# q for two groups at a time, w1 in one block of columns, outputs picked by one masked product and one sum, four unit products fewer

## The chip, the cores and the metric

The kernel runs on one core of one Trainium2 chip. A core has a matrix engine (PE; its weight loads are shown as PEld), a vector engine (DVE), an engine for activation functions (ACT), GpSimd (POOL) and an engine that here only issues transfers (SP). They work side by side and wait for each other through semaphores. 16 DMA engines bring data from HBM into the on-chip memory (SBUF, 128 partitions); PE writes its results into eight banks of PSUM. The metric is the device time of one execution in microseconds, lower is better; the time before is a median of three runs.

## The reference

Two layers, each an attention step of a decoder with cached keys and values and a gated feed-forward, on 4 sequences with one token each:

```python
B, D, Hq, Hkv, Sk, Dh, F = 4, 512, 32, 8, 4096, 128, 1792
def A(x, k_cache, v_cache, wq, wo):
    q = (x @ wq).reshape(B, 1, Hq, Dh).transpose(0, 2, 1, 3)
    k, v = repeat(k_cache, 4, axis=1), repeat(v_cache, 4, axis=1)
    p = softmax(einsum("bhqd,bhkd->bhqk", q, k) * Dh ** -0.5)
    return einsum("bhqk,bhkd->bhqd", p, v).transpose(0, 2, 1, 3).reshape(B, 1, Hq * Dh) @ wo
def F_(x, w1, w3, w2):
    return (silu(x @ w1) * (x @ w3)) @ w2
for layer in range(2):
    x = x + A(layernorm(x), k_cache, v_cache, wq, wo)
    x = x + F_(layernorm(x), w1, w3, w2)
```

Both layers use the same weights and the same caches, all in float32. Keys and values are 4 x 8 x 4096 x 128 numbers each, 134 MB together; a layer needs them once.

## The kernel before

**Loads.** The host lays keys, values and all weights side by side into one array `rows` of 128 partitions. The table `LOADS` lists 87 transfers from it into one large SBUF tile, `space`, as (first unit, count, place), a unit being 256 columns of float32. `pump` (L125) issues them in that order, on SP, each as soon as its places are free; `done` (L158) frees places after the last instruction that reads them, and calls `pump`. SP runs in order: a transfer whose place is not free holds back all behind it. Some data of layer 0 stays in `space` for layer 1 (w1, half of the last group's keys and values, part of wq, wo and w2), and layer 1 goes through the groups in reverse.

**Attention.** A group is one of the 8 key heads with its 4 query heads. Per group (loop at L587) `score` multiplies the keys of 2048 positions with q (16 tiles of 512 columns for 4 sequences, four row blocks of 32 side by side on PE), `maximum` and `exponent` take the softmax of it without its division, `turn` transposes p into pT, all this twice; then `weigh` multiplies the values (twice 16 matmuls into the two banks `o_ps[0]` and `o_ps[1]`). `join_maxima` and `join_sums` make the factors that put the partial softmaxes together, and `finish` (L424) picks the four blocks that belong together out of each bank, one factor and one DVE instruction per block: four of bank 0 stand beside the second `weigh`, four of bank 1 behind it. `turn_o` and `gather_o` stand inside the next group's scores, after 8 and after 12 of its 16 matmuls.

**q.** While a group runs, q of the next one is made: `share_q` (four matmuls of the four 128-row pieces of x, into the four row blocks of the bank `wide`), `take_q` (one DVE pass that scales them), `turn_q` (four matmuls that add the pieces and transpose, within the second scores), `copy_q` (into `qT`).

**Feed-forward** (L480). w1 and w3 stand in two blocks of columns, "a" (256) and "b" (192); 4 x 4 matmuls each fill one block of the banks `gate` and `up`. `swish` is a sigmoid on ACT and a product on DVE, `times_up` another product, `turn_h` transposes h, `down` multiplies w2, 14 chunks of 16 small matmuls. `hum` multiplies a unit matrix into a bank that nothing reads; `busy` does the same at the end of an attention. `factor` makes the reciprocal deviation of the layer norm: matmuls that sum squares (`mean`, L233), one DVE instruction (L256), one on POOL (L257).

The order on each engine is the order of the code. A tile is the unit of the waits that are put in: an instruction that writes a tile waits for readers of other parts of it, where the engine has not waited for a later one yet.

Of the kernel before, what the change touches and what calls it, by code (L numbers as in the profile page):

```python
# [15 lines left out]
REP = HQ // HKV  # L16
# [54 lines left out]
SCRATCH = 64  # L71

# [5 lines left out]
def tile_decode_layers(ctx: ExitStack, tc: tile.TileContext, rows, out):  # L78
# [29 lines left out]
    for kind, n in (("w1a", KC), ("w1b", KC), ("w3a", KC), ("w3b", KC), ("w2", 14)):  # L108
        stream += [(kind, k) for k in range(n)]
    size = {"wq": HOME, "wo": HOME, "kv": U // KB, "w2": D // KB}  # L110
    for kind in ("w1", "w3"):
        size[kind + "a"], size[kind + "b"] = 4 * HALF // KB, 4 * (FJ - HALF) // KB
# [45 lines left out]
    def done(layer, *key):  # L158
        if layer == 0 and (key[0][:2] == "w1" or key[0] in ("wq", "wo") and key[1] >= HELD or key[:2] == ("kv", TURN) and key[2] in KEPT or key[0] == "w2" and key[1] >= LASTS):
            return  # L160
# [18 lines left out]
    rowsum, ssq, ve, rstd = columns[:, 4:5], columns[:, 5:6], columns[:, 6:8], columns[:, 8:10]  # L179
    alike, other = columns[:, 12:12 + REP], columns[:, 12 + REP:12 + 2 * REP]  # L180
# [13 lines left out]
    qT = const.tile([P, B, 32 + LEAD], F32, name="qT")  # L194
    nc.vector.memset(qT, 0.0)
    sums_ps = psum.tile([P, KC, P], F32, name="sums_ps")
# [40 lines left out]

    def deviation():
# [7 lines left out]
    def lay_down(xin):  # L246
        xT = work.tile([P, P], F32, name="xT", bufs=1)
        nc.vector.transpose(xT, xin)
        return xT
# [9 lines left out]
    def layernorm():  # L259
        xc, sq = deviation()  # L260
        xT = lay_down(xc)
# [7 lines left out]
        return xT, factor  # L269
# [9 lines left out]
    def turn_over(g):  # L279
        xT = lay_down(x_ps)  # L280
# [3 lines left out]
        for k in range(KC):  # L284
            for i in range(KC):
                nc.tensor.matmul(q_ps[32 * i:32 * i + 32, :].rearrange("p (h c) -> p h c", h=REP),
                                 xT[:, 32 * k:32 * k + 32], w[:, k, i], start=(k == 0), stop=(k == KC - 1))
# [4 lines left out]
        nc.vector.tensor_scalar(qT[:, :, LEAD:].rearrange("p b (t r) -> p b t r", t=2)[:, :, :, 0:REP],  # L292
                                q.unsqueeze(2).to_broadcast([P, B, 2, REP]), SCALE, None, op0=ALU.mult)
        xc, sq = deviation()
        xT = lay_down(xc)
        squares(xc, sq)

        def factor():
# [4 lines left out]
            inverse(rstd, o_ps[1][:, 1:3])  # L303

        return xT, factor


    def copy_q(q=None):
        q = misc[:, 0:B * REP].rearrange("p (h b) -> p b h", h=REP) if q is None else q
        nc.vector.tensor_copy(qT[:, :, LEAD:].rearrange("p b (t r) -> p b t r", t=2)[:, :, :, 0:REP],  # L310
                              q.unsqueeze(2).to_broadcast([P, B, 2, REP]))
# [11 lines left out]
    def take_q(rstd):  # L323
        shares = work.tile([P, REP * DH], F32, name="shares", tag="p", bufs=1)
        nc.vector.tensor_scalar(shares, wide, rstd, -D * SCALE, op0=ALU.mult, op1=ALU.mult)  # L325
# [9 lines left out]
    def score(layer, g, c, between={}):  # L335
        ps = scores()
        order = (2, 3, 4, 5, 6, 7, 0, 1) if layer and (g, c) == (TURN, STORED) else range(TILES)
        for m, r in enumerate(order):
            key = "kv", g, TILES * c + r
            t = loaded(*key)  # L340
            at = LEAD - REP * (r // 2)
# [338 lines left out]
```

## Time and profile before

| | |
|---|---|
| median of 3 runs | 702.99 us (702.89 to 703.22) |
| the profiled execution | 703.43 us |
| its span, first to last instruction | 701.6 us |
| mean granted clock of PE | 0.827 |
| read from HBM | 296.81 MB, 423 GB/s over the span |
| busiest line of PE | L349, scores: 164.8 us in 1024 records |
| second | L413, values: 151.0 us in 1024 records |

The page gives busy time per engine, the transfers per queue, the chain of work that ended last, and groups of equal instructions as: line, engine, operation, output <- inputs, shape, count | busy us, mean ns of one | idle time of the engine before them, and what ended it. A matmul of float32 stands as two records with a weight load each. Granted clock is the share of full speed at which PE ran. In a timeline row the first two numbers are start and duration in us, and the bracket is the idle time before it and what ended that.

### The profile page before, as it was taken

To read this page: it belongs to the slowest core of one execution; us is meant where nothing else is said; L and a number is where in the kernel's file an instruction comes from. 1 tells how busy PE (TensorE), PEld (TensorE's weight loads), DVE (VectorE), ACT (ScalarE), POOL (GpSimd) and SP (SyncE) were. 2 spreads that over 40 slices of the span, in tenths; PEclk is the share of its full clock that TensorE was granted. 3 is DMA by queue.
4 is the path that set the end of the run, shared out by engine and by line. 5 is a ranking of instruction groups with operands and counts; after the bars stand their busy time and mean duration, and the time that the engine had idled before them with its cause. 6 is when DMAs were issued, how large, how long until landed. Compare 5 with 4: busy or idle time off the path is not lost.

```text
span 701.6 us, 7504 instructions
## 1 busy us (share of the span) xinstructions
PE 415.9 (59%) x3280; PEld 134.2 (19%) x3280; DVE 144.5 (21%) x512; ACT 43.2 (6%) x106; POOL 3.1 (0%) x10
## 2 busy tenths in 40 slices
PE   1255566554675519566587995644654725567577
PEld 0111121111221103121134231211211201111124
DVE  2012121121120203231221332112111401212322
ACT  0010000000000001010201210000100001000100
POOL 0000000000000000000000000000000000000000
PEclk9997677866787669887999998787868958778989
DMA  9999999999999999999999999999999999999996
GB/s 407 433 419 418 467 423 418 427 453 430 418 423 461 414 441 414 429 432 427 418 422 367 425 432 433 444 427 426 453 422 428 444 424 429 434 441 416 424 422 263
DMA packets 12703, 297.34 MB, mean 424 GB/s; under 512 B 1408, under 2 KB 1536, under 8 KB 4480
## 3 DMA queue, kind: packets, MB, share of 16 engines
q1 hardware_dynamic: 12672, 296.88, 98.9%
q8 instruction: 25, 0.41, 0.2%
q14 instruction: 6, 0.05, 0.0%
HBM read 296.81 MB, written 0.07 MB: 423 GB/s over the span
## 4 chain that ended last, share of the span: by engine, by line
DMA 72%; PE 24%; DVE 2%; another core or an unknown queue 1%; issue 1%; ACT 0%; SPq 0%; DVEq 0%; ACTq 0%
DMA space<-in_rows 72%; PE o L413 14%; PE scores L349 6%; PE turned L374 1%; PE o L489 1%; DVE pT L376 1%; PE sums_ps L330 1%; DVE o L436 0%; ACT p L367 0%; PE sums_ps L533 0%; DVE acc L361 0%; PE sums_ps L457 0%; SPq L149 0%; PE scores L230 0%
## 5 line engine op out<-in xcount | busy, mean ns | idle before, releaser
L349 PE MATMUL scores<-space,qT 128*32 128x512 f32 x1024 | 164.8, 699 | 138.6 <-DMA space<-in_rows 137.9
L413 PE MATMUL o<-space,pT 128*16 128x512 f32 x1024 | 151.0, 711 | 105.3 <-DMA space<-in_rows 99.1
L349 PEld LDWEIGHTS scores<-space,qT 128*32 128x32 f32 x1024 | 35.0, 120 | 212.2 <-issue 176.6
L413 PEld LDWEIGHTS o<-space,pT 128*16 128x16 f32 x1024 | 32.9, 109 | 204.9 <-issue 101.2
L361 DVE TENSOR_REDUCE acc<-scores 128x1 f32<-128x512 f32 x32 | 22.1, 692 | 177.3 <-PE scores L349 177.3
L367 ACT ACTIVATE p<-scores,acc 128x512 f32<-128x512 f32 x30 | 20.6, 687 | 556.7 <-DVE acc L361 422.9
L436 DVE SCALAR_TENSOR_TENSOR o<-o,acc,o 128x128 f32<-128x128 f32 x112 | 39.3, 351 | 48.9 <-PE o L413 45.5
L376 DVE COPY pT<-turned 128x256 f32<-128x256 f32 x32 | 13.6, 425 | 162.2 <-PE turned L374 162.2
L374 PE MATMUL turned<-ident,p 128*128 128x128 f32 x128 | 23.3, 310 | 12.1 <-ACT p L367 12.1
L374 PEld LDWEIGHTS turned<-ident,p 128*128 128x128 f32 x128 | 14.9, 152 | 44.4 <-ACT p L367 26.3
L447 DVE COPY o<-sums_ps 128x16 f32<-128x16 f32 x16 | 2.8, 175 | 95.7 <-PE sums_ps L446 95.7
L319 PE MATMUL sums_ps<-space,xT 128*32 128x512 f32 x120 | 20.8, 715 | 2.8 <-DMA space<-in_rows 2.8
L330 PEld LDWEIGHTS sums_ps<-same,shares 128*128 128x128 f32 x120 | 15.6, 203 | 16.6 <-DVE shares L325 11.1
L330 PE MATMUL sums_ps<-same,shares 128*128 128x4 f32 x120 | 16.9, 264 | 0.9 <-DVE shares L325 0.9
L489 PE MATMUL o<-space,xT 128*32 128x192 f32 (+1 forms) x256 | 13.9, 355 | 3.5 <-DVE h L509 1.6
L467 PE MATMUL stored<-space,o 128*32 128x512 f32 x104 | 13.5, 592 | 0.0
L325 DVE TENSOR_SCALAR shares<-sums_ps,columns 128x512 f32<-128x512 f32 x15 | 11.1, 743 | 1.7 <-PE sums_ps L319 1.7
L533 PE MATMUL sums_ps<-space,hT 128*4 128x128 f32 x224 | 9.3, 292 | 2.8 <-DMA space<-in_rows 2.4
L235 PE MATMUL o<-columns,same 128*32 128x1 f32 x64 | 2.0, 181 | 14.8 <-DVE columns L578 13.8
L446 PEld LDWEIGHTS sums_ps<-columns,o 128*128 128x128 f32 x32 | 5.5, 218 | 20.7 <-issue 14.5
L489 PEld LDWEIGHTS o<-space,xT 128*32 128x32 f32 x256 | 7.7, 110 | 8.6 <-DVE h L509 2.6
L446 PE MATMUL sums_ps<-columns,o 128*128 128x16 f32 x32 | 7.1, 299 | 1.2 <-DVE o L436 1.2
(105 smaller groups left out, 142.9 us busy)
## 6 DMA issues: line engine op xcount, KB each, us to landing
space<-in_rows SPq DMA_DIRECT2D x7, 4096.0 KB, 25.8
space<-in_rows SPq DMA_DIRECT2D x3, 6144.0 KB, 31.8
space<-in_rows SPq DMA_DIRECT2D x8, 2048.0 KB, 25.1
space<-in_rows SPq DMA_DIRECT2D x2, 7168.0 KB, 41.8
space<-in_rows SPq DMA_DIRECT2D x4, 3072.0 KB, 26.6
space<-in_rows SPq DMA_DIRECT2D x11, 1024.0 KB, 13.4
space<-in_rows SPq DMA_DIRECT2D x3, 3584.0 KB, 17.7
space<-in_rows SPq DMA_DIRECT2D x2, 5120.0 KB, 21.4
```

The lines of the kernel that those rows point to most:

```text
L319: nc.tensor.matmul(wide[32 * k:32 * k + 32, :], xT[:, 32 * k:32 * k + 32], w[:, k, :], start=True, stop=True)
L330: nc.tensor.matmul(misc[:, h * B:(h + 1) * B], shares[:, h * DH:(h + 1) * DH], same[:, 0:B], start=True, stop=True)
L349: nc.tensor.matmul(ps[32 * b:32 * b + 32, :], qT[:, b, at:at + 32], u, start=(m < 2), stop=(m >= TILES - 2))
L361: nc.vector.tensor_reduce(acc[:, i:i + 1], ps, axis=AX.X, op=ALU.max, negate=True)
L367: nc.scalar.activation(p.rearrange("p n s -> p (n s)"), ps, AF.Exp, bias=acc[:, i:i + 1], scale=1.0 if scale is None else scale, accum_out ...
L374: nc.tensor.transpose(pt[:, n, :], p[:, n, :], ident)
L376: nc.vector.tensor_copy(pT, pt.rearrange("p n (b r) -> p n b r", b=B)[:, :, :, 0:ROW])
L413: nc.tensor.matmul(o_ps[i][32 * b:32 * b + ROW, :], pT[:, r // 2, b, :], t[:, j * NB * DH:(j + 1) * NB * DH], start=(r < 2), stop=(r >= TI ...
L436: nc.vector.scalar_tensor_tensor(o, o_ps[s][:, j * DH:(j + 1) * DH], acc[:, 16 + NB * s + j:17 + NB * s + j], o, op0=ALU.mult, op1=ALU.add)
L446: nc.tensor.matmul(misc[:, 0:B * REP], o, head, start=True, stop=True)
L467: nc.tensor.matmul(bank[32 * h:32 * h + 32, :], oT[:, h, :], w[:, h, :], start=first, stop=last)
L489: nc.tensor.matmul(bank[32 * j:32 * j + 32, s], xT[:, 32 * k:32 * k + 32], w[:, j], start=(k == 0), stop=(k == KC - 1))
```

## The change

- `share_q`, `take_q`, `turn_q` and `copy_q` take a list of one or two groups (`SHARED`). Two groups share the bank: the second one's x is read four columns earlier (`window`), so it lands in other rows of each block; one pass and one set of four `turn_q` matmuls serve both. Fifteen rounds become eight.
- w1 is one block of 448 columns; sigmoid and product take it whole in both layers. Two entries of `LOADS` are cut differently.
- `o_ps[0]` and `o_ps[1]` become one tile, `o_all`. In `finish`, but for a layer's last group, one DVE product multiplies both banks with the factors in place and one sum over the eight blocks gives o, both behind the second `weigh`.
- In `down`, the four `hum` of layer 0 go; one of the three `hum` before it goes with w1's second block. In layer 0, three chunks of w3's block "b" stand ahead of `turn_h(0)` for one.
- The first pT of each group is copied by ACT for DVE. `qT`, `oT` and `xT` are set up once; `wo` products are 8 columns wide for 32 and 4.

```diff
-    (1180, 16, 144), (1152, 16, 0), (1168, 12, 16), (1196, 3, 161), (1199, 3, 145), (1202, 3, 148), (1205, 3, 151),
+    (1180, 16, 144), (1152, 21, 0), (1173, 7, 21), (1196, 3, 161), (1199, 3, 145), (1202, 3, 148), (1205, 3, 151),
...
+SHARED = ({-1: (0, 1), 1: (2, 3), 3: (4, 5), 5: (6, 7)}, {0: (6,), 1: (5, 4), 3: (3, 2), 5: (1, 0)})
+PAD = B
+WIDE = 2 * B
...
-    o_ps = [psum.tile([P, NB * DH], F32, name=f"o{i}", tag=f"o{i}") for i in range(STEPS)]
-    for i in range(STEPS):
-        nc.vector.memset(o_ps[i], 0.0)
+    o_all = psum.tile([P, STEPS, NB * DH], F32, name="o_all")
+    nc.vector.memset(o_all, 0.0)
+    o_ps = [o_all[:, i] for i in range(STEPS)]
...
+    def window(k, j=0):
+        at = PAD + 32 * k - B * j
+        return xT[:, at:at + 32]
...
-    def share_q(layer, g, xT):
-        w = wq_of(g)
-        for k in range(KC):
-            nc.tensor.matmul(wide[32 * k:32 * k + 32, :], xT[:, 32 * k:32 * k + 32], w[:, k, :],
-                             start=True, stop=True)
-        done(layer, "wq", g)
+    def share_q(layer, gs):
+        for j, g in enumerate(gs):
+            w = wq_of(g)
+            for k in range(KC):
+                nc.tensor.matmul(wide[32 * k:32 * k + 32, :], window(k, j), w[:, k, :],
+                                 start=(j == 0), stop=(j == len(gs) - 1))
+        for g in gs:
+            done(layer, "wq", g)
+
+    def spread_out():
+        rows = across(rstd[:, 0:1])[:, 0:B]
+        nc.vector.scalar_tensor_tensor(rows, rows, 1.0, alike, op0=ALU.mult, op1=ALU.mult, accum_out=spread)
...
-    def turn_q(shares):
+    def turn_q(shares, n):
         for h in range(REP):
-            nc.tensor.matmul(misc[:, h * B:(h + 1) * B], shares[:, h * DH:(h + 1) * DH], same[:, 0:B],
+            nc.tensor.matmul(misc[:, h * n * B:(h + 1) * n * B], shares[:, h * DH:(h + 1) * DH], same[:, 0:n * B],
                              start=True, stop=True)
...
-        nc.vector.tensor_copy(pT, pt.rearrange("p n (b r) -> p n b r", b=B)[:, :, :, 0:ROW])
+        copy(pT, pt.rearrange("p n (b r) -> p n b r", b=B)[:, :, :, 0:ROW])
...
-        nc.vector.memset(oT, 0.0)
+        o = work.tile([P, DH], F32, name="o", tag="p", bufs=1)
+        if not at_end:
+            weigh(layer, g, c, 1, pT)
+            blocks = o_all.rearrange("p i (j d) -> p (i j) d", j=NB)
+            nc.vector.tensor_tensor(blocks, blocks, acc[:, 16:24].unsqueeze(2).to_broadcast([P, 2 * NB, DH]), op=ALU.mult)
+            nc.vector.tensor_reduce(o, blocks.rearrange("p j d -> p d j"), axis=AX.X, op=ALU.add)
+            return o
...
-                if layer == 0 and m in (1, 3, 8, 11):
-                    hum(2 if m < 5 else 0, 1)
...
-            part(gate, "w1a")
-            hum(1, 3)
-            swish(cols["a"])
+            part(gate, "w1")
+            swish(every)
+            nc.scalar.activation(spare, half[:, 0:1], AF.Exp)
             times_up(cols["a"])
-            part(gate, "w1b")
-            swish(cols["b"])
-            nc.scalar.activation(spare, half[:, 0:1], AF.Exp)
-            part(up, "w3b", (0,))
+            part(up, "w3b", (0, 1, 2))
             turn_h(0)
-            part(up, "w3b", (1, 2, 3))
+            part(up, "w3b", (3,))
...
-            part(gate, "w1a", (0,))
+            part(gate, "w1", (0,))
             factor()
-            part(gate, "w1a", range(1, KC))
-            part(gate, "w1b")
-            swish(slice(0, FJ))
+            part(gate, "w1", range(1, KC))
+            swish(every)
             part(up, "w3a")
```

**Three places in the built order.** PE in layer 0's feed-forward, from w3's block "a" on, before (a row is line, operation, output <- inputs, shape of the output and count; in this layer `o_94` is up and `o_95` gate):

```order
L489 MATMUL o_94<-space,xT 32x256 x12
L494 MATMUL sums_ps<-space,ident 128x128
L497 MATMUL scores<-ident 128x384
L489 MATMUL o_95<-space,xT 32x256 x16
L497 MATMUL scores<-ident 128x384
L489 MATMUL o_95<-space,xT 32x192 x16
L489 MATMUL o_94<-space,xT 32x192 x4
L514 MATMUL scores<-ident,h 128x128 x2
L489 MATMUL o_94<-space,xT 32x192 x12
```

and the same place in the changed kernel:

```order
L515 MATMUL o_all<-space,xT 32x256 x12
L520 MATMUL sums_ps<-space,ident 128x128
L523 MATMUL scores<-ident 128x384
L515 MATMUL o_all<-space,xT 32x448 x16
L515 MATMUL o_all<-space,xT 32x192 x12
L540 MATMUL scores<-ident,h 128x128 x2
L515 MATMUL o_all<-space,xT 32x192 x4
```

The two w1 blocks of 16 matmuls are one, a unit product between them is gone, and the transposes of h moved behind the third chunk of w3's block "b".

PE in layer 1's feed-forward, from the sums of squares to the second block of w3, with the semaphores that a row waits for, before (here `o_94` is gate and `o_95` up, which also holds the variance):

```order
L235 MATMUL o_95<-columns,same 32x1 [waits DVE_49]
L235 MATMUL o_95<-columns,same 32x1 x3
L489 MATMUL o_94<-space,xT 32x256 x12
L489 MATMUL o_94<-space,xT 32x192 x16
L489 MATMUL o_95<-space,xT 32x256 [waits DMAHW7_49,DVE_49]
L489 MATMUL o_95<-space,xT 32x256 x15
L489 MATMUL o_95<-space,xT 32x192 [waits DMAHW0_49,DVE_49]
```

and in the changed kernel:

```order
L246 MATMUL o_all<-columns,same 32x1 [waits DVE_49]
L246 MATMUL o_all<-columns,same 32x1 x3
L515 MATMUL o_all<-space,xT 32x448 [waits DVE_49]
L515 MATMUL o_all<-space,xT 32x448 x11
L515 MATMUL o_all<-space,xT 32x256 [waits DMAHW7_49,DVE_49]
L515 MATMUL o_all<-space,xT 32x256 x15
L515 MATMUL o_all<-space,xT 32x192 [waits DMAHW0_49,DVE_49]
```

A wait for DVE is new ahead of w1's second chunk: its count is that of the variance's reading (L269). Ahead of w3's first block DVE was waited for before too, but for the variance's reading (L256); now the count is that of the gate's product (L532).

DVE at a group's end, from the reciprocal of the sum to the copy of the turned output, before:

```order
L400 RECIPROCAL acc<-acc 128x1
L401 TENSOR_SCALAR acc<-acc 128x2
L402 TENSOR_TENSOR acc<-columns,acc 128x8
L431 MEMSET o 128x128
L432 TENSOR_SCALAR o<-o_94,acc 128x128
L436 SCALAR_TENSOR_TENSOR o<-o_94,acc,o 128x128 x3
L436 SCALAR_TENSOR_TENSOR o<-o_95,acc,o 128x128 x4
L447 COPY o<-sums_ps 128x4x4
```

and in the changed kernel:

```order
L419 RECIPROCAL acc<-acc 128x1
L420 SCALAR_TENSOR_TENSOR acc<-columns,acc 128x8
L452 TENSOR_TENSOR o_all<-o_all,acc 128x1024
L453 TENSOR_REDUCE o<-o_all 128x128
L471 COPY oT<-sums_ps 128x4x4
```

Eight picks and a clearing became two instructions over both banks; a layer's last group keeps the eight.

More of the change, by code (lines that the diff above doesn't have):

```diff
@@ L422, in store_last, with finish @@
         done(0, *key)
-    def finish(layer, g, c, p, acc):
-        pT = turn(p)
+    def finish(layer, g, c, p, acc, at_end):
+        pT = turn(p, nc.vector.tensor_copy)
         if (layer, g) == (0, TURN):
@@ L461, in project_o, with gather_o @@
                                        accum_out=rowsum)
-    def gather_o(layer, g, oT, bank, first=True, last=True):
+    def gather_o(layer, g, bank, first=True, last=True):
         w = wo_of(g)
         for h in range(REP):
-            nc.tensor.matmul(bank[32 * h:32 * h + 32, :], oT[:, h, :], w[:, h, :], start=first, stop=last)
+            nc.tensor.matmul(bank[32 * h:32 * h + WIDE, :], oT[:, h, :], w[:, h, :], start=first, stop=last)
         done(layer, "wo", g)
@@ L476, in add_o, with feed_forward @@
         for k in range(KC):
[L477 removed]
+            nc.tensor.matmul(x_ps[32 * k:32 * k + WIDE, :], same[:, 0:WIDE], shares[:, k * P:(k + 1) * P],
+                             start=True, stop=True)
         nc.vector.tensor_tensor(x_sb, x_ps, x_sb, op=ALU.add)
[L480 removed]
+    def feed_forward(layer, factor):
         gate, up = o_ps if layer else o_ps[::-1]
         cols = {"a": slice(0, HALF), "b": slice(HALF, FJ)}
+        every = slice(0, FJ)
         def part(bank, kind, ks=range(KC)):
[L485 removed]
+            s = every if kind == "w1" else cols[kind[2]]
             for k in ks:
@@ L598, in tile_decode_layers @@
                 pump()
-            pT = turn(p)
+            pT = turn(p, nc.scalar.copy)
             between = {}
-            if n + 1 < len(order):
-                shares = take_q(rstd[:, 0:1])
-                between[2] = lambda shares=shares: turn_q(shares)
+            if n in shared:
+                shares = take_q()
+                between[2] = lambda shares=shares, n=len(gs): turn_q(shares, n)
             if layer == 0 and n == TURN - 2:
```

124 lines of the change are left out of this document (65 added, 59 removed).

## The prediction

> **What bounds the kernel now.** I read the page first, then the stages, then the two places where transfers are not deep in a queue.
>
> ```profile
> span 701.6 us, 7504 instructions
> PE 415.9 (59%) x3280; PEld 134.2 (19%) x3280; DVE 144.5 (21%) x512; ACT 43.2 (6%) x106; POOL 3.1 (0%) x10
> ...
> q1 hardware_dynamic: 12672, 296.88, 98.9%
> q8 instruction: 25, 0.41, 0.2%
> ...
> DMA 72%; PE 24%; DVE 2%; another core or an unknown queue 1%; issue 1%; ACT 0%; SPq 0%; DVEq 0%; ACTq 0%
> ```
>
> The reader is to see that no compute engine is busy for two thirds of the span, while the packets of one queue, the loads into `space`, fill 98.9% of all 16 DMA engines' time. The chain of waits (the last line) is DMA for 72%. The 24% of PE in it says little: the chain steps onto PE wherever a load was issued when PE released its place, even if older loads were still running.
>
> ```profile
> 5.00:360.00 355.00, 200.17 (x1360) 60.83 (x1364) 68.69 (x235) 19.32 (x49) 0.55 (x1) 0.81 1.00 432
> 360.00:385.00 25.00, 19.92 (x334) 11.24 (x323) 4.14 (x17) 2.75 (x6) 0.55 (x1) 0.93 0.98 379
> 385.00:690.00 305.00, 188.53 (x1437) 58.11 (x1441) 66.16 (x241) 19.83 (x50) 1.25 (x2) 0.83 1.00 430
> 690.00:701.60 11.60, 7.27 (x165) 4.05 (x157) 2.30 (x8) 0.00 (x0) 0.00 (x0) 1.00 0.49 189
> ```
>
> These windows (length; busy time of PE, PEld, DVE, ACT and POOL; granted clock; DMA share; GB/s) cut the span into layer 0's attention, layer 0's feed-forward, layer 1's attention and the end. Through 660 of 702 us the DMA share is 1.00 at 430 to 432 GB/s. So nothing saved on PE, DVE or ACT in the attention can show, as long as loads are issued before the queue runs dry. Two places remain: the feed-forward at 360 to 385 (0.98, 379 GB/s) and the end.
>
> **The change, part by part.** The loads carry the same bytes: the two loads of w1 (16 and 12 units of 256 columns) become 21 and 7, again 28. So the 296.88 MB and their time stay.
>
> *Attention.* Fifteen rounds of q become eight, and each spares four matmuls that turn the shares; ACT takes 16 copies of pT from DVE; eight DVE instructions at a group's end become a product over 1024 columns and a sum over as many. The trace has neither of the last two; the nearest rows are these.
>
> ```profile
> L361 DVE TENSOR_REDUCE acc<-scores 128x1 f32<-128x512 f32 x32 | 22.1, 692 | 177.3 <-PE scores L349 177.3
> L436 DVE SCALAR_TENSOR_TENSOR o<-o,acc,o 128x128 f32<-128x128 f32 x112 | 39.3, 351 | 48.9 <-PE o L413 45.5
> L276 DVE TENSOR_TENSOR space<-space,stored 128x2048 f32<-128x2048 f32 x1 | 2.3, 2290 | 7.2 <-PE stored L275 7.2
> ```
>
> A reduction of 512 took 0.69 us and a product of 2048 took 2.29 us, so the pair lies between 2 x 0.69 = 1.4 and 2 x 2.29 = 4.6 us; by columns it is 1.15 + 1.25 = 2.4 us, which I take. It starts only when the last weighted V matmul is done; before, four of the eight pieces (4 x 0.36 = 1.5 us) came that late. So o is ready 0.9 us later (0 to 3.1). Behind it on DVE stands the next maximum, on PE the turning of o after eight score matmuls. In 14 of 16 groups PE has idle time to spare. In the dense start of layer 1 it costs PE under a microsecond, against this:
>
> ```profile
> space<-in_rows SPq DMA_DIRECT2D x1, 512.0 KB, 5.2
> ...
> space<-in_rows SPq DMA_DIRECT2D x1, 1024.0 KB, 6.7
> ```
>
> These are the single issues at 370.9 and at 384.7, with their time to landing. At 424 GB/s their own bytes take 1.2 and 2.5 us, so each stood some 4 us behind older loads: that is the cover of every delay of a release, and the least I found. Attention: 0.
>
> *Layer 0's feed-forward.* Five unit products go, w1 runs in one block, and the third matrix's second block (w3b) now waits for sigmoid, gate product and up product of the whole block.
>
> ```profile
> 369.02 1.83 PE L489 MATMUL o<-space,xT 128*32 128x192 f32 x40 [0.95 <-DVE h L509]
> 370.59 0.42 ACT L505 ACTIVATE h<-o,columns 128x192 f32<-128x192 f32 x1 [2.74 <-PE o L489]
> ...
> 374.70 1.03 PE L533 MATMUL sums_ps<-space,hT 128*4 128x128 f32 x16 [0.95 <-DMA space<-in_rows]
> ...
> 375.66 0.80 PE L497 MATMUL scores<-ident 128*128 128x128 f32 x2
> ...
> 378.06 0.62 PE L533 MATMUL sums_ps<-space,hT 128*4 128x128 f32 x16
> ```
>
> Before, w3b's first chunk ends with the first row, at 370.85, and the issue at 370.9 follows. Now w1's last chunk is done at about 369.8; sigmoid 0.63, product 0.68 and up product 0.48 us (rows below) with gaps make 1.9, so w3b starts near 371.8 and its first release comes at 372.3, 1.4 us later than before. The issue had 4 us in hand and keeps 2.6. The engines are not equally far along, though: 379 GB/s says that some ran dry here already. Bounds: 0, and 1.4 if all run dry for it; I take 0.1, near the queue's 4 us. The unit products left out (0.8 us in the row, four among the down products) let PE release w2's places earlier, which pays that back.
>
> On the clock, the two rows of 16 down products show 1.03 and 0.62 us. The Trainium skill (TensorE: Matmul & The Clock Gate, Part 1: The HAM clock gate) says that PE falls to half rate after about 3.4 us of idling, which speaks against leaving out unit products. By that rule each pair of w2 chunks would take 1.03 us, by the fast row 0.62; two chunks are 512 KB, 1.2 us of transfer, so the sum stays 0 either way.
>
> *The end.* Here the changed order counts. The two banks of o are one tile now, and the built order makes PE wait: w1's second chunk for the reading of the variance, w3's first block for the gate's product.
>
> ```profile
> 679.84 0.13 PEld L413 LDWEIGHTS o<-space,pT 128*16 128x16 f32 x8 [0.85 <-DMA space<-in_rows]
> ...
> 686.32 4.51 PE L489 MATMUL o<-space,xT 128*32 128x256 f32 x88
> 686.60 0.16 DVE L256 TENSOR_SCALAR columns<-o 128x1 f32<-128x1 f32 x1 [0.67 <-PE o L235]
> ...
> 689.25 0.63 ACT L505 ACTIVATE h<-o,columns 128x448 f32<-128x448 f32 x1 [22.60 <-PE o L489]
> 689.92 0.68 DVE L506 SCALAR_TENSOR_TENSOR h<-o,columns,h 128x448 f32<-128x448 f32 x1 [3.16 <-ACT h L505]
> 690.89 0.48 DVE L509 SCALAR_TENSOR_TENSOR h<-o,columns,h 128x256 f32<-128x256 f32 x1 [0.29 <-PE o L489]
> 691.43 1.51 PE L489 MATMUL o<-space,xT 128*32 128x192 f32 x32 [0.61 <-DVE h L509]
> ...
> 693.59 0.62 PE L533 MATMUL sums_ps<-space,hT 128*4 128x128 f32 x16 [0.28 <-DVE hT L515]
> ...
> 695.92 1.06 PE L533 MATMUL sums_ps<-space,hT 128*4 128x128 f32 x32 [0.24 <-DMA space<-in_rows]
> 697.18 1.06 PE L533 MATMUL sums_ps<-space,hT 128*4 128x128 f32 x24 [0.20 <-DMA space<-in_rows]
> 698.49 0.40 PE L533 MATMUL sums_ps<-space,hT 128*4 128x128 f32 x8 [0.25 <-DMA space<-in_rows]
> ```
>
> The second row is 44 matmuls with 10,240 columns in 4.51 us: 0.44 ns a column. w1's first chunk has 448 columns for 256, so the variance comes 4 x 192 x 0.44 = 0.34 us later and is read until 687.1; then 12 x 448 columns take 2.4 us, and sigmoid starts at 689.74, 0.49 late. Sigmoid and product (1.35 with the gaps) end at 691.1. Only then w3's first block runs, 1.8 us that lay beside them before; up product 0.5, second block and transposes 2.16 as before: the down products start at 695.7 instead of 693.59, **2.1 us late**. PE's waits for loads behind that point (0.24 + 0.20 + 0.25 = 0.7) absorb a third. So the last product would end **1.4 us** later, if the chain started at the same time. (0 if PE did not wait, which the order excludes.)
>
> But the chain starts with loads: the first row waits for one. That is where instructions come in. PE runs 6560 of them (line 1), 25 packets of 0.41 MB on the instruction queue: one of 16 KB per some 256. The change drops 65 of 1709 matmuls, some 260 instructions: one packet, and each packet after that comes later.
>
> ```profile
> q8 instruction: 1, 0.02, 22.1%
> ```
>
> ```profile
> space<-in_rows SPq DMA_DIRECT2D x1, 4096.0 KB, 19.8
> ...
> space<-in_rows SPq DMA_DIRECT2D x1, 3072.0 KB, 31.2
> ...
> space<-in_rows SPq DMA_DIRECT2D x1, 4096.0 KB, 37.9
> ...
> space<-in_rows SPq DMA_DIRECT2D x1, 35.0
> ```
>
> One packet falls at 663 (first fence). The 4096 KB issued at 650.12 landed 19.8 us later, at 669.9, its predecessor (issued 628.04) at 659.2: 10.7 us for it. The same size issued at 458.48 landed at 496.4, after 486.7: 9.7 us. A packet on the DMA engine that is last thus costs all that follows up to **1.0 us**, and PE's final chain starts on the load that paid it. Counting PE's instructions in both orders, a packet per 256, the one at 663 (last group's scores) moves into the last projection, near 684: behind the start of the chain. Bounds: 0, and -1.0; I take -1.0, the row itself. A load behind it may still be late by it, but the last one lands at 698.45, and PE is by then the later of the two. The Trainium skill (Runtime: NRT & Kernel Launch, Instruction fetch mechanics) has the 16 KiB blocks of 256 instructions, as the count here agrees, and calls crossing one "mostly hidden"; by that rule the term is 0 and the end 1.4 us late.
>
> Sum against the profiled run (703.43 us: the span of 701.6 and 1.83 around it): 0 + 0.1 + 1.4 - 1.0 = +0.5, less some 0.2 for places released earlier without unit products: **+0.3 us**. The median of the three runs is 702.99, 0.44 below the profiled one; so **703.3 us**.
>
> **Rivals.**
> - *The late end without relief*, ending slower. If the packet does not move, or another DMA engine is just as late, the sum is 0.1 + 1.4 - 0.2 = +1.3 us: 704.3, on the edge of slower. It decides where the chain's earlier start falls to nothing; each tenth that the waits of 0.7 us absorb less then takes it over the edge. For it: only one interval shows a packet's price, and 15 other engines are close. Against: the row of 1.06 us for 24 records hides a further gap, so the waits may be longer than I counted. 0.25. The skill's rule on crossing a block, above, would end here.
> - *The queue runs dry in layer 0*, slower. If w3b's release comes over 4 us late instead of 1.4, each microsecond more is lost whole. For it: 379 GB/s, so little is in hand. Against: 2.6 us left by my count. With partly dry engines and the late end it is 705. 0.05.
> - *Packets fall better*, faster. One packet less on the last engine and none moved onto it gives -1.0 with the end's waits absorbed better than I count (+0.4): 702.4; over -1.4 only with a second packet gone. 0.2, a quarter of it below 701.6.
> - *The change doesn't do what it says*: engine work falls and the time stays exactly. This is within my forecast, 0.5.
>
> **How the numbers follow.** 0.2%, about what a measurement of this kernel can tell from no change, is 1.4 us: 701.6 to 704.4. Slower: half of the late end and all of the dry queue, 0.17. Faster: 0.05. Same: 0.78. The range takes in the better packets and the late end with 0.2 above it: 702.2 to 704.6.
>
> **What would show it.** The instruction queue should hold 24 packets; the loads' share should stay near 99% and the attention windows at 430 to 432 GB/s. At the end the gate's product should stand between w1 and w3 on PE, w3 waiting for it about 1.3 us, and the last down products should no longer wait for loads. The load that ends the last group's V wait should land nearer 669 than 669.9. A DMA share under 0.95 at 370 to 376 would make me wrong in layer 0; a final chain that starts as late as before would make the end's price 1.4.

## The result, and the profile after

| | before | after |
|---|---|---|
| median | 703.01 us (4 runs, 702.89 to 703.22) | 709.42 us (4 runs, 708.97 to 714.19) |
| ratio, 95% interval | | 1.0106 [1.0063, 1.0149] |
| measured again, beside other versions | 702.93 us (23 runs) | 709.56 us (6 runs, 707.48 to 712.42), 1.0093 [1.0075, 1.011] |
| profiled execution, its span | 703.43, 701.6 | 708.97, 707.2 |

The change costs 6.4 us, where 0.3 had been forecast. The four executions of the changed kernel lie up to 5 us apart, where four of before lie within 0.5 and the 23 of the later series within 2.

The page of the changed kernel (span; busy time; the queues of loads and of instructions; the chain):

```profile
span 707.2 us, 7145 instructions
PE 408.8 (58%) x3150; PEld 125.7 (18%) x3150; DVE 127.3 (18%) x382; ACT 48.9 (7%) x121; POOL 3.1 (0%) x10
...
q1 hardware_dynamic: 12672, 296.88, 98.4%
q8 instruction: 24, 0.39, 0.2%
...
DMA 65%; PE 29%; DVE 3%; another core or an unknown queue 1%; issue 1%; ACT 0%; SPq 0%; DVEq 0%; ACTq 0%
L452 DVE TENSOR_TENSOR o_all<-o_all,acc 128x1024 f32<-128x1024 f32 x14 | 17.3, 1233 | 58.8 <-PE o_all L432 58.8
...
L453 DVE TENSOR_REDUCE o<-o_all 128x128 f32<-128x1024 f32 x14 | 17.1, 1225 | 0.5
```

PE, DVE and the instruction queue do less, as the change says, and the span is 5.6 us longer. The same bytes are loaded, over more time: the loads' share falls, PE's share of the chain grows by 5 points. To find the place, the windows of before that the prediction did not show (columns as there; the last three are granted clock, DMA share, GB/s):

```profile
370.00:375.00 5.00, 3.48 (x59) 1.69 (x52) 0.93 (x3) 1.91 (x3) 0.00 (x0) 0.96 0.91 349
...
385.00:390.00 5.00, 4.58 (x56) 1.30 (x56) 1.79 (x8) 1.81 (x5) 0.70 (x1) 1.00 1.02 418
390.00:395.00 5.00, 3.79 (x32) 1.94 (x32) 1.32 (x4) 1.84 (x4) 0.00 (x0) 1.00 1.04 428
...
360.00:405.00 45.00, 37.78 (x498) 17.14 (x491) 11.95 (x48) 7.50 (x18) 1.25 (x2) 0.96 1.00 399
```

and of the changed kernel:

```profile
370.00:375.00 5.00, 2.92 (x39) 1.18 (x34) 1.36 (x3) 2.12 (x3) 0.00 (x0) 0.82 0.61 206
...
385.00:390.00 5.00, 3.87 (x56) 2.35 (x56) 1.61 (x7) 0.37 (x2) 0.00 (x0) 0.50 1.00 377
390.00:395.00 5.00, 5.00 (x52) 1.41 (x44) 0.80 (x5) 1.81 (x5) 0.70 (x1) 0.63 0.90 329
...
360.00:405.00 45.00, 35.38 (x441) 15.50 (x442) 8.99 (x36) 8.37 (x21) 1.25 (x2) 0.85 0.94 358
```

From 360 to 405 the share is 0.94 for 1.00: 45 x 0.06 = 2.7 us of loading are lost, mostly at 370 to 375 (0.61) and, behind a granted clock of 0.50 and 0.63, at 390 to 395 (0.90). From 405 to 690 both have 1.00 at 431 GB/s. The last load lands at 701.62 for 698.45, **3.2 us later**. The output is issued 3.21 us behind that, where 0.83 stood before: **2.4 us more at the end**. Together 5.6, the whole difference of the spans.

PE's timeline in the changed kernel, at the last group of layer 0, in its feed-forward, and at the first scores of layer 1:

```profile
352.93 5.19 PE L432 MATMUL o_all<-space,pT 128*16 128x512 f32 x32 [3.34 <-DVE o L459]
...
367.16 3.21 PE L515 MATMUL o_all<-space,xT 128*32 128x448 f32 x32
372.45 1.48 PE L515 MATMUL o_all<-space,xT 128*32 128x192 f32 x24 [2.08 <-DVE h L535]
...
388.20 3.64 PE L368 MATMUL scores<-space,qT 128*32 128x512 f32 x16 [0.69 <-DVE qT L305]
```

and the same scores before:

```profile
385.42 1.92 PE L349 MATMUL scores<-space,qT 128*32 128x512 f32 x16 [0.72 <-DVE qT L292]
```

The first row is a wait that the prediction did not see: the second value product writes bank 1 of `o_all`, and waits for DVE's picks of bank 0 (L459, the instructions that take the four blocks that belong together out of a bank), the same tile. The row of the scores shows what a clock of 0.50 means: 16 records in 3.64 us for 1.92. Before, the same product waited for its loads in layer 0 and for pT in layer 1, and in layer 1 the picks of bank 0 ran beside it:

```profile
350.55 4.46 PE L413 MATMUL o<-space,pT 128*16 128x512 f32 x24 [2.52 <-DMA space<-in_rows]
355.41 1.05 PE L413 MATMUL o<-space,pT 128*16 128x512 f32 x8 [0.40 <-DMA space<-in_rows]
...
677.14 3.75 PE L413 MATMUL o<-space,pT 128*16 128x512 f32 x32 [0.52 <-DVE pT L376]
...
678.91 1.12 DVE L436 SCALAR_TENSOR_TENSOR o<-o,acc,o 128x128 f32<-128x128 f32 x3
```

And the end of the changed kernel:

```profile
682.01 3.63 PE L432 MATMUL o_all<-space,pT 128*16 128x512 f32 x32 [3.33 <-DVE o L459]
...
694.50 0.64 ACT L531 ACTIVATE h<-o_all,columns 128x448 f32<-128x448 f32 x1 [22.79 <-PE o_all L515]
...
695.91 1.93 PE L515 MATMUL o_all<-space,xT 128*32 128x256 f32 x32 [1.56 <-DVE h L532]
...
700.61 0.62 PE L559 MATMUL sums_ps<-space,hT 128*4 128x128 f32 x16 [0.28 <-DVE hT L541]
...
701.63 2.80 PE L559 MATMUL sums_ps<-space,hT 128*4 128x128 f32 x96
...
704.83 0.35 SPq L657 DMA_DIRECT2D out<-space  x1
```

The same wait (3.33 us), then w3 behind the gate's product (1.56), then 96 down products in one piece: they no longer wait for loads, PE is the later of the two.

### The profile page after: what moved, and what is told of

It is laid out like the page before. It is cut to its first block, busy times and chain, and to the rows that moved or that the text cites. A ratio compares the mean times of both kernels' runs of the same rounds, so it can differ in the third digit from the quotient of the medians.

```text
span 707.2 us, 7145 instructions
## 1 busy us (share of the span) xinstructions
PE 408.8 (58%) x3150; PEld 125.7 (18%) x3150; DVE 127.3 (18%) x382; ACT 48.9 (7%) x121; POOL 3.1 (0%) x10
## 4 chain that ended last, share of the span: by engine, by line
DMA 65%; PE 29%; DVE 3%; another core or an unknown queue 1%; issue 1%; ACT 0%; SPq 0%; DVEq 0%; ACTq 0%
DMA space<-in_rows 65%; PE o_all L432 15%; PE scores L368 6%; PE o_all L515 2%; PE turned L393 1%; PE sums_ps L559 1%; DVE pT L395 1%; DVE o L459 1%; PE sums_ps L349 1%; PE stored L288 1%; PE sums_ps L333 0%; PE sums_ps L481 0%; PE scores L299 0%; ACT p L386 0%
## 5 line engine op out<-in xcount | busy, mean ns | idle before, releaser
L432 PE MATMUL o_all<-space,pT 128*16 128x512 f32 x1024 | 148.1, 704 | 109.2 <-DMA space<-in_rows 96.1
L432 PEld LDWEIGHTS o_all<-space,pT 128*16 128x16 f32 x1024 | 32.7, 108 | 205.4 <-issue 156.2
L395 DVE COPY pT<-turned 128x256 f32<-128x256 f32 x16 | 6.8, 425 | 136.6 <-PE turned L393 136.6
L452 DVE TENSOR_TENSOR o_all<-o_all,acc 128x1024 f32<-128x1024 f32 x14 | 17.3, 1233 | 58.8 <-PE o_all L432 58.8
L515 PE MATMUL o_all<-space,xT 128*32 128x256 f32 (+2 forms) x192 | 14.6, 434 | 6.1 <-DVE h L535 2.7
L453 DVE TENSOR_REDUCE o<-o_all 128x128 f32<-128x1024 f32 x14 | 17.1, 1225 | 0.5
L491 PE MATMUL stored<-space,oT 128*8 128x512 f32 x104 | 13.5, 592 | 0.0
L349 PEld LDWEIGHTS sums_ps<-same,shares 128*128 128x128 f32 x64 | 8.6, 208 | 9.9 <-DVE shares L344 6.8
L344 DVE TENSOR_SCALAR shares<-sums_ps,columns 128x512 f32<-128x512 f32 x8 | 6.0, 751 | 22.1 <-PE turned L393 20.0
L349 PE MATMUL sums_ps<-same,shares 128*128 128x8 f32 (+1 forms) x64 | 9.3, 271 | 0.9 <-DVE shares L344 0.9
```

The lines of the kernel that those rows point to most:

```text
L349: nc.tensor.matmul(misc[:, h * n * B:(h + 1) * n * B], shares[:, h * DH:(h + 1) * DH], same[:, 0:n * B], start=True, stop=True)
L432: nc.tensor.matmul(o_ps[i][32 * b:32 * b + ROW, :], pT[:, r // 2, b, :], t[:, j * NB * DH:(j + 1) * NB * DH], start=(r < 2), stop=(r >= TI ...
L452: nc.vector.tensor_tensor(blocks, blocks, acc[:, 16:24].unsqueeze(2).to_broadcast([P, 2 * NB, DH]), op=ALU.mult)
L453: nc.vector.tensor_reduce(o, blocks.rearrange("p j d -> p d j"), axis=AX.X, op=ALU.add)
L515: nc.tensor.matmul(bank[32 * j:32 * j + 32, s], window(k), w[:, j], start=(k == 0), stop=(k == KC - 1))
```

## The experiments

Three suspects: the one tile (T), the unit products left out (U), w1 in one block (W). In the table, "units" are the unit products and "picks" the eight DVE instructions per group. The last two columns are the DMA share from 360 to 405 and the time from the last load's landing to the output's issue, both in the one execution that was profiled. For e2 that was the slowest of four (708.70 us) and for e3 the fastest (708.78), so their traces and medians don't describe the same execution.

| kernel | median us | ratio to before [95%] | share | end |
|---|---|---|---|---|
| before | 703.0 | | 1.00 | 0.83 |
| after | 709.4 | 1.0106 [1.0063, 1.0149] | 0.94 | 3.21 |
| g3_after_again: the same kernel | 709.56 | 1.0093 [1.0075, 1.011] | 0.96 | 4.03 |
| e1_units: after + units | 711.3 | 1.0108 [1.0089, 1.0126] | 0.94 | 5.16 |
| e2_two_tiles: after, two tiles, picks | 707.05 | 1.0058 [1.0043, 1.0073] | 0.91 | 0.83 |
| e3_w1_blocks: after, w1 in blocks | 711.23 | 1.0113 [1.0086, 1.0141] | 0.95 | 3.69 |
| e4_before_no_units | 703.06 | 1.0003 [0.9994, 1.0013] | 1.00 | 0.83 |
| f1_tiles_blocks: e2 and e3 together | 705.08 | 1.0031 [1.0019, 1.0043] | 0.98 | 0.83 |
| f2_per_bank: f1, product and sum per bank | 703.81 | 1.0015 [1.0001, 1.0029] | 1.00 | 0.83 |
| f3_before_w1_whole | 704.66 | 1.0025 [1.0015, 1.0035] | 0.96 | 0.83 |
| f4_product_at_end: after, no picks at all | 711.65 | 1.0119 [1.0099, 1.0139] | 0.91 | 3.57 |
| g1_before_one_tile: product and sum too | 711.15 | 1.0107 [1.0085, 1.0129] | 0.92 | 4.83 |
| g2_per_bank_units: f2 + units | 702.83 | 1.0002 [0.9993, 1.001] | 1.01 | 0.83 |
| g4_picks_units: f1 + units | 703.71 | 1.0014 [1.0002, 1.0026] | 0.99 | 0.83 |
| h1_after_units_in_wait | 708.4 | 1.0077 [1.0065, 1.0089] | 0.96 | 4.40 |
| h2_one_tile_units_in_wait: g1 + units | 707.62 | 1.0072 [1.006, 1.0085] | 0.98 | 3.90 |
| h3_w1_whole_even_loads: f3, other loads | 705.77 | 1.0039 [1.0026, 1.0052] | 0.95 | 0.83 |

One column is exact: every kernel with two tiles issues its output 0.83 us behind the last load, every kernel with one tile 3.2 to 5.2 us behind it.

**The unit products alone.** Back in the changed kernel:

```diff
                 done(layer, "w2", m)
+                if layer == 0 and m in (1, 3, 8, 11):
+                    hum(2 if m < 5 else 0, 1)
```

> The changed kernel with the four unit products back among layer 0's down products, nothing else. Theory U (the unit products kept PE's clock up): the granted clock at 385 to 395 is 1.00 again where it was 0.50 and 0.63, the scores there take 1.9 us for 16 and not 3.6, the loads that were issued late behind them come earlier, and some 2 us of the 6.4 are back: about 707.4 us. Theory T (one tile for both banks makes the start and the end late, and the clock falls because PE then waits for loads): the clock stays near half there and the time at 709.4, at most 0.5 below.

and out of the kernel before (the same lines removed):

> The kernel before without the four unit products among layer 0's down products, nothing else. Theory U: the granted clock at 385 to 395 falls from 1.00 to 0.5 to 0.7 and the time rises by some 2 us, to 705. Rival (the clock fell because loads came late, so PE stood idle): the clock stays at 1.00 and the time at 703.0, within 0.3.

Both misses for U: 711.3 with them (clock 0.50 and 0.69 at 385 to 395 all the same; its interval lies within that of the changed kernel), 703.06 without. They are neither the cause nor, alone, worth anything.

**One tile.** Two tiles again in the changed kernel, which brings the eight picks back:

```diff
-    o_all = psum.tile([P, STEPS, NB * DH], F32, name="o_all")
-    nc.vector.memset(o_all, 0.0)
-    o_ps = [o_all[:, i] for i in range(STEPS)]
+    o_ps = [psum.tile([P, NB * DH], F32, name=f"o{i}", tag=f"o{i}") for i in range(STEPS)]
+    for i in range(STEPS):
+        nc.vector.memset(o_ps[i], 0.0)
...
-        if not at_end:
...
```

> The changed kernel with two tiles for the two banks and the eight picks in every group, as before; q in pairs, w1 in one block and the missing unit products stay. Theory T: the second value product of a layer's last group no longer waits for the picks of the first bank (3.33 us in layer 1), nor w3's first block for the gate's product (1.56 us); the end gives back the 2.4 us by which it is later than the last load, and layer 0's feed-forward starts 1.7 us earlier, of which 0 to 1.7 show: 705.5 to 707. Theory U alone: the waits go, the time stays within 1 us of 709.4, since the loads set the end.

707.05, at the upper edge of what T allowed: the end's lateness is gone (0.83), as T says. But in the profiled execution the queue runs drier than in the changed kernel (0.91), and the last load lands at 703.72 for 701.62. There w1 waits for its load, and behind that wait its 32 records take 4.91 us, for 3.21 in the changed kernel:

```profile
366.82 4.91 PE L509 MATMUL o<-space,xT 128*32 128x448 f32 x32 [1.79 <-DMA space<-in_rows]
```

So the earlier start brings nothing in this execution. The reverse, one tile and the product and sum put into the kernel before:

> The kernel before with one tile for both banks and the masked product and one sum in all but the last groups; w1 in two blocks, q per group and the four unit products stay as before. Theory (one tile costs at two places): layer 0's feed-forward starts 1.7 us later, w3's second block waits for the gate's product, the issue of 370.9 comes at about 373.7 and some 2 us are lost there; the end comes 2.4 us later than the last load would let it: 707 to 708.5. Rival (only the end is late, the start is covered): 705.4.

711.15, 8.2 us more, over what T allowed: **one tile, with the product and sum that need it, costs as much as the whole change** (ratio 1.0107 beside 1.0106). The product and sum themselves are not seen to cost: they run in all groups but the last ones, and from 5 to 350 and from 405 to 690 the DMA share is 1.00 at 431 GB/s, as before. The changed kernel itself, run again for comparison:

> The changed kernel itself once more, beside these versions on one chip. 709.4 is expected, with executions between 708.8 and 714: where its times lie above the profiled 709, PE's clock at 360 to 400 and the loads issued there will differ, not the attention.

709.56, and its end took 4.03 us. The clock from 385 to 395 was 0.77 and 1.00 in this profiled execution, for 0.50 and 0.63 in the first, and the share from 360 to 405 was 0.96 for 0.94. The span is nearly the same (707.0 and 707.2), so the low clock at that place is not what the 6.4 us hang on.

**w1 in one block.** Undone in the changed kernel (load sizes, host layout and feed-forward as before):

```diff
-    (1180, 16, 144), (1152, 21, 0), (1173, 7, 21),
+    (1180, 16, 144), (1152, 16, 0), (1168, 12, 16),
...
-            part(gate, "w1")
-            swish(every)
+            part(gate, "w1a")
+            hum(1, 3)
+            swish(cols["a"])
...
```

> The changed kernel with w1 in two blocks of columns again (loads, host layout and the order of the feed-forward as before, with the one unit product between the blocks); the one tile and the missing four unit products stay. Theory W (w3's first release behind the whole swish lets the queue run dry): the issue at 373.05 moves to about 372 (the feed-forward still starts 1.7 us late), the DMA share of 370 to 375 rises from 0.61 to 0.75 or more, and about 1 us is back, with up to 0.5 at the end: 708 to 708.4. If the queue was dry for the late start alone: 709 to 709.4.

A miss: 711.23, though its executions, from 708.78 to 713.55, leave some 2 us either way open. With one tile, w3's second block waits for DVE in either form. In its trace the block starts at 373.13, for 372.45, behind the gate's product (L533), and the share from 370 to 375 is 0.52:

```profile
373.13 0.53 PE L516 MATMUL o_all<-space,xT 128*32 128x192 f32 x8 [0.99 <-DVE h L533]
```

Done alone in the kernel before (the reverse edit):

> The kernel before with w1 in one block of columns, in loads (21 and 7 units for 16 and 12), host layout and the order of the feed-forward; two tiles and eight picks stay, the four unit products too. Theory: this alone is over half of the loss. w1's first matmul waits for a load that lands 1.5 us later (366.7 for 365.2), PE stands idle 1.8 us and its clock falls, w1 takes up to 4.9 us for 3.2, w3's second block starts near 373.8, the issue of 370.9 comes at 372.5 to 374.7 and the DMA share of 370 to 375 falls to 0.4 to 0.6: 705 to 707. Rival (the 4 us of cover that the prediction counted hold): 703.0 to 703.5.

704.66, 1.65 us more: real, but under the 705 to 707 that were expected, and not over half. The timeline of this kernel:

```profile
366.90 3.21 PE L488 MATMUL o<-space,xT 128*32 128x448 f32 x32 [1.77 <-DMA space<-in_rows]
372.18 1.18 PE L488 MATMUL o<-space,xT 128*32 128x192 f32 x24 [2.07 <-DVE h L508]
```

and its window:

```profile
370.00:375.00 5.00, 2.78 (x50) 1.56 (x50) 1.78 (x4) 2.12 (x3) 0.00 (x0) 1.00 0.65 232
```

The issue of 370.90 comes at 372.77, and the share falls from 0.91 to 0.65: 5 x 0.26 = 1.3 us of loading. Is it the larger first load, or the release behind the whole swish? Only the loads changed:

```diff
-    (1152, 21, 0), (1173, 7, 21)
+    (1152, 14, 0), (1166, 14, 14)
```

> The kernel before with w1 in one block (704.66 us), its two loads cut at 14 and 14 units for 21 and 7. If what w1's one block costs is mostly that its first matmul waits 1.77 us for a load that lands at 366.76, the load now lands at about 365, w1 runs 1.5 us earlier, the issue at 372.77 comes near 371.3 and the time is 703 to 703.7. If it is the first release behind the whole swish, it stays at 704.2 to 704.7.

```profile
364.88 1.71 PE L488 MATMUL o<-space,xT 128*32 128x448 f32 x16
368.81 2.04 PE L488 MATMUL o<-space,xT 128*32 128x448 f32 x16 [2.23 <-DMA space<-in_rows]
372.91 2.15 PE L488 MATMUL o<-space,xT 128*32 128x192 f32 x24 [2.06 <-DVE h L508]
```

705.77, above both ranges: the first half starts 2 us earlier, the second waits for the other load, and w3 is no earlier. So it is not the larger first load. It is the release behind the swish, which needs all of w1, and w1's last load lands near 369 in either cut (368.99 and 368.77), as it did before (368.89). The 1.1 us more than with the first cut are not clear of noise, since the two intervals overlap.

**Everything else.** Two tiles and w1 in blocks:

> The changed kernel with two tiles and eight picks, and with w1 in two blocks of columns; what stays of the change is q for two groups at a time, the first pT copied by ACT, the narrower products, and the four unit products left out. Theory: one tile and w1's one block are the whole loss together (each alone undone gave back 2.4 and nothing, because the other still lets the queue run dry at 370 to 375): 703.0, within 0.5; DMA share at 370 to 375 back at 0.9, granted clock 1.00 at 385 to 395. Rival (q in pairs or ACT's copies cost something of their own): 704 to 706, with the share below 0.8 somewhere else.

and the product and sum kept, one pair per bank:

```diff
+            for s in range(STEPS):
+                if s:
+                    weigh(layer, g, c, 1, pT)
+                blocks = o_ps[s].rearrange("p (j d) -> p j d", j=NB)
+                nc.vector.tensor_tensor(blocks, blocks, ..., op=ALU.mult)
+                nc.vector.tensor_reduce(both[:, s], blocks.rearrange("p j d -> p d j"), axis=AX.X, op=ALU.add)
+            nc.vector.tensor_tensor(o, o, both[:, 1], op=ALU.add)
```

> As the kernel with two tiles and w1 in two blocks, but the outputs picked by a masked product and a sum per bank (and one addition of the two sums) in all but the last groups, so that the part of the first bank stands beside the second value product. Theory: the idea of product and sum costs nothing, only the one tile did: 703.0, within 0.5, the same as with eight picks. Rival (the product and the sum behind the second value product delay the next group's releases and the queue): 0.5 to 1.5 us above the version with picks.

705.08 and 703.81, both above the 703.0 within 0.5 that was expected: most is back, not all, and product and sum are no worse than picks. The rest was tried with the unit products, on the second and on the first:

> As the version with two tiles, w1 in two blocks and a product and a sum per bank, with the four unit products back. Theory U2 (what is left there, 0.8 us, is the granted clock of 0.81 to 0.85 at 380 to 390, which unit products keep up): clock 1.00 there and 703.0, within 0.3. Rival (the rest is where instruction packets fall, or q in pairs): 703.8, unchanged.

> As the version with two tiles, eight picks and w1 in two blocks, with the four unit products back. Theory U2: the granted clock at 385 to 390, 0.66 without them, is back near 1.00, the scores there are 1 us faster and the time is 703.0 to 704. Rival (units do nothing here either; the 2.1 us of that version are loads that a packet made late): 705.1.

702.83, the time of before, and 703.71, both as U2 says. The windows of the version at 702.83:

```profile
385.00:390.00 5.00, 4.62 (x56) 1.15 (x52) 2.05 (x10) 1.95 (x6) 0.70 (x1) 1.00 1.02 411
390.00:395.00 5.00, 4.22 (x32) 2.06 (x36) 0.75 (x1) 1.96 (x5) 0.00 (x0) 1.00 1.03 427
```

The clock, 0.66 at 385 to 390 in f1 and 0.81 in f2, is 1.00. The gains, 1.4 and 1.0 us, are of the size of the intervals, so that the units give them is likely, not settled. What is settled by the version at 702.83 (1.0002 [0.9993, 1.001]): q in pairs, ACT's copies and product and sum together cost nothing, and gain nothing. The one at 703.71, with picks, lies just above 1 (from 1.0002). No version beat the kernel before.

**Taking the picks away.** Product and sum in the last groups too, so that nothing stands between the two value products:

```diff
-        if not at_end:
+        if True:
```

> The changed kernel with the masked product and the one sum in a layer's last group too, so that no picks of the first bank stand between the two value products; one tile, w1 in one block and all else stay. Theory (the second value product of the last group waited 3.33 us for picks that only share its tile): it starts as soon as its weights and loads are there, 1.5 to 2.5 us earlier; the sum costs 2.46 us behind it for 1.4 of four picks; the end comes 0.5 to 1.5 us earlier: 708 to 709. Layer 0 gains nothing, since w1's load lands at 366.6 anyway. Rival (the lateness of the loads sets the end): 709.4, or 1 us more for the longer sum.

A miss: 711.65, with an interval that overlaps the changed kernel's. The value product of layer 0 does start early and ends at 356.5, but behind it stand 2.46 us of product and sum, 1.56 of them with PE idle, the clock is 0.65 and 0.67 from 360 to 370, and the issue of 370.90 comes at 374.87.

**Wait or clock?** PE kept busy in the wait, in the changed kernel and in g1:

```diff
         add(0, range(1, NB))
+        busy(4)
+        busy(4)
         weigh(layer, g, c, 1, pT)
```

> The changed kernel with two unit products of 512 columns each on PE ahead of the second value product of a layer's last group, where PE waits 3.33 us for the picks of the other bank; nothing else. Theory C (part of the cost of that wait is the clock behind it: the 32 records took 5.0 to 5.3 us in layer 0 where 4.0 to 4.4 stood before): they take about 4.2 us, the feed-forward starts 0.8 us earlier, the times lie closer together (none above 711) and the median is 708 to 709. Theory W (only the wait counts): 709.5, with the same spread of 707.5 to 712.

> The kernel before with one tile (711.15 us), with the same two unit products in the wait of the last groups. There the 32 records behind the wait of 3.47 us took 6.51 us in layer 0 at a granted clock of 0.61, and 5.32 in layer 1. Theory C: 4.2 and 4.2 us, the issue that came at 375.31 comes at about 373.5, the end 1 us earlier: 708 to 709. Theory W: 711, within 0.5.

708.4, as theory C says, and 707.62, below its range. In g1 3.5 us come back (the intervals only touch), in the changed kernel 1.1 (they overlap), so that a gain is likely and its size open. The second value product of layer 0, in g1, five of whose six times ran from 707 to 713:

```profile
353.02 6.51 PE L413 MATMUL o_all<-space,pT 128*16 128x512 f32 x32 [3.47 <-DVE o L442]
```

and with units in the wait (h2, whose times end at 710):

```profile
352.52 3.85 PE L413 MATMUL o_all<-space,pT 128*16 128x512 f32 x32 [0.91 <-DVE o L442]
356.30 1.13 PE L230 MATMUL scores<-ident 128*128 128x512 f32 x2
```

Now it ends at 356.3, as in the kernel before (356.4), though it still waits for the picks: the values of this group land at 355.3 anyway. In layer 0 the wait itself is covered, and its price in this row is the clock behind it. At the end of layer 1 it is not: h2 still issues its output 3.90 us behind the last load.

## Why the prediction was wrong, step by step

- *"Attention: 0", and the built order read at three places only.* This is the step that failed. The order of the last group, where the eight picks stay, was not read, though the kernel's rule stood in the text: a tile is the unit of the waits. So the second value product's wait for the first bank's picks (3.34 and 3.33 us) was missed in both layers, and with it a term of some 2 us at the end. In layer 1, its pT is there at 679.2 and it starts at 682.0; had it started then, it would have waited for its last load (682.5) and ended near 683.6, not at 685.6: an estimate of 2.0 us from these rows and the 1.05 us of the last 8 records before. In layer 0 it ends at 358.05 for 356.4, 1.65 us, and that is clock: with PE kept busy in the wait it ended at 356.4 too.
- *The clock rule, weighed for the down products only.* After waits of 3.33 to 3.47 us the same 32 records took between 3.63 and 6.51 us (3.63, 4.97, 5.19 and 5.32 among them), and 3.63 to 3.86 with PE kept busy in the wait. The Trainium skill (TensorE: Matmul & The Clock Gate, Part 1: The HAM clock gate) has a window of about 3.4 us that runs free of the kernel; by it, a wait near that length may fill one or not, from run to run. The scatter agrees with that. One row of the kernel before does not: behind 2.52 us of waiting its clock from 350 to 355 was 0.66. The prediction applied the rule where loads hide it and did not ask where else PE would newly stand idle.
- *w3b's release, "1.4 us later", of 4 us in hand: 0.1.* The delay was near (1.87 with w1's one block alone, 2.15 in the changed kernel), the cover was not there. It was counted to the landing of the queue's last load, but the share of 0.91 before shows that engines ran dry already; what is later is lost nearly whole: 1.65 us alone (f3). The sign that the prediction named, a share under 0.95 there, came (0.61), but the kernel before was under it too.
- *The end, +2.1 for sigmoid and gate.* Right: sigmoid is 5.25 us late and the down products 7.02, of which w1's start has 4.75; so 0.50 and 1.77, 2.27 together. w3 waits 1.56 us, 1.3 were forecast, and the down products no longer wait for loads, which absorbed 1.46 (0.7 forecast). The chain's start failed: 4.75 us later instead of 1.0 earlier, some 2.7 of it loads that landed later and 2.0 the wait for the picks.
- *A packet moved, -1.0.* It did not move. The queues of the changed kernel between 660 and 667 (packets, MB, share) still show one:

```profile
q1 hardware_dynamic: 109, 3.09, 103.0%
q8 instruction: 1, 0.02, 1.0%
```

  and the last group's loads are late by what was lost at 360 to 405: the load that was to land nearer 669 than 669.9 landed at 672.63. The price of 1.0 rested on one interval of 10.7 us and did not come again: with a packet in it, the same interval took 9.9 us in the changed kernel (662.70 to 672.63) and 9.7 in e4_before_no_units (659.27 to 668.99). The count was right: 24 packets.
- *q in pairs, the copy on ACT, product and sum (2.4 forecast, 1.23 + 1.23 measured).* Right: with two tiles and w1 in blocks, and the units back, 702.83 us.
- *The rivals.* "The late end without relief" (0.25) named part of the mechanism and priced it at 1 us; "the queue runs dry in layer 0" (0.05) had the place, and that its sum of 705 is near w1's one block alone is luck: it asked for a release over 4 us late, and 1.87 were enough. That both come together with a slower clock was not among the cases, and the range ended 5 us too low.

How the 6.4 us split: undone alone, one tile gives back 2.4 and w1's one block nothing that can be told from the scatter, and in both traces w3 still waits for DVE; done alone, they cost 8.2 and 1.65. Undone together they give back 4.3, and with the four unit products 5.7 (with picks) or 6.6 (product and sum per bank). These parts do not add up, and the table is the answer rather than a sum. How much of them is the slower clock stays open.

## What to carry to other kernels

Before two buffers are joined, list for every engine what writes one part while another engine reads the other; each such pair becomes a wait, also in code that the change leaves as it is. Price a new wait by two things, who is behind it and whether PE stands idle long enough to lose its clock. Cover is what the transfer engines still have to do, not the time until the last load lands; here the share of 0.91 said that it was used up.

## What the runs showed of the hardware

- Two banks need no such wait: with two tiles DVE reads one bank while PE writes the other (the rows of before at 677.14 and 678.91). The Trainium skill (PSUM — Partial Sum Buffer, PSUM bank collisions raise a hardware error) says the same, that accesses to different banks run clean; the wait came from the tile, not from the chip.
- The clock also fell without a wait of 3 us: in the changed kernel to 0.50 at 385 to 390, where PE's gaps from 376 on were 1.2 us at most. The window ahead of it, there:

```profile
380.00:385.00 5.00, 2.37 (x48) 1.02 (x48) 0.00 (x0) 0.00 (x0) 0.00 (x0) 0.84 1.01 381
```

  and in the kernel before without units, where the clock stayed:

```profile
380.00:385.00 5.00, 2.63 (x76) 1.70 (x76) 1.02 (x4) 0.37 (x2) 0.00 (x0) 1.00 1.02 397
385.00:390.00 5.00, 4.55 (x56) 1.12 (x48) 1.60 (x7) 1.97 (x6) 0.70 (x1) 1.00 1.02 413
```

  2.37 and 2.63 us of 5 busy, 0.50 and 1.00 behind it: what counts there stays open.
